# Casting the weight differences one block later, and forming the four sums of the second MLP's input in two steps

## The chip, the core and the metric

The program runs on one core of one Trainium2 chip. The metric is the device time of one execution in microseconds (us); lower is better. In the text PE is the matrix engine (TensorE), DVE is VectorE, ACT is ScalarE and POOL is GpSimd. Each engine works through its own queue in order; DVE, ACT and POOL hand results to each other and to PE through semaphores.

## What is computed

Rotary attention over 4 batches x 8 heads x 576 positions x 64, then two MLPs on its output, a matrix of 2304 x 512, all in float32:

```python
    gate = 1.0 / (1.0 + np.exp(-(x @ w_gate)))        # first MLP, d_ff 1536
    val = x @ w_val
    x = (gate * val @ w_out)
    h = x @ w_in                                      # second MLP, d_ff 2048
    g = h * (1.0 / (1.0 + np.exp(-1.702 * h)))
    return (g @ w_out).astype(np.float32)
```

The weights arrive as 64-bit numbers and are decoded to float32 on the chip.

## The kernel before

**Split products.** PE multiplies in the fp32r format, so each operand is held as a high part (a rounded copy) and a low part (the rest), and each product takes three matmuls: low x high, high x low, high x high (`split_mm`, L539; `product`, L614). The high part is made by a copy (ACT or DVE), the low part by a subtraction, mostly on POOL.

**Loops.** The hidden width is cut into chunks of 256 columns: six chunks (1, 0) to (1, 5) of the first MLP, eight chunks (2, 0) to (2, 7) of the second. The 2304 tokens are five blocks, 0 to 3 of 512 and 4 of 256. The order is written by hand: for a chunk, block after block, `hidden` (psum tiles `psh`, activation into `g`, L569 to L572) is issued, then the output product of an earlier block (`out1` or `out2`; psum tiles `pso`, added to `acc` by DVE, L693 or L710/L712), then the decoding of one piece of the next chunk's weights. There are four `psh` and four `pso` buffers: PE can run ahead of DVE by as much.

**A chunk of the second MLP** goes as follows. Blocks 0 and 1 are done together by `hidden_pair`: seven products of six matmuls, by a scheme that uses differences of the weight blocks (`Weights.differences`) and sums of the input blocks (`pair_sums`) in place of eight products. Then PE does, in this order, out2(4) of the chunk ahead, hidden(2), out2(0), hidden(3), out2(1), hidden(4), out2(2), out2(3), and the next chunk's pair. The numbers in brackets are blocks.

**Decoding.** `decode(i)` of a piece of 128x512: a copy on ACT into `wc` (L179), five DVE operations (L186 to L192; the last makes the high part of the weight), and POOL's subtraction for the low part (L210). Pieces 0 and 1 of a second-MLP chunk are the input weights; they stay in two `wt` buffers. With piece 1 (issued after out2(0) in a second-MLP chunk, after out1(0) in chunk (1, 5)) comes `differences`: four POOL subtractions on the two `wt` buffers (L202), then for each buffer a cast on ACT (L206) and a low part on POOL (L207). `wt` has two buffers in all, so piece 2 writes into the one that the first cast and its low part have read.

**The sums.** In chunk (1, 5) `out1` finishes the first MLP's output in `acc`. Behind out1(1) `pair_sums` forms four sums of 128x1024 on DVE (L601), casts each on ACT (L602) and makes each low part on POOL (L603). `hidden_pair` of chunk (2, 0) reads them.

Of the kernel before, what the change touches and what calls it, by code (L numbers as in the profile page):

```python
# [9 lines left out]
F32R = mybir.dt.float32r  # L10
U32 = mybir.dt.uint32
AF = mybir.ActivationFunctionType
ALU = mybir.AluOpType
# [13 lines left out]
def f(ap):  # L27
    return ap.bitcast(F32)
# [3 lines left out]
def attention_then_mlps(  # L32
# [86 lines left out]
            return a.rearrange("p (f w) -> p f w", w=2) if tag == "raw" else a  # L119

    stage = [Spare()]
    wpools = [big, None]
    wts = {}

    class Weights:
# [70 lines left out]
        def differences(self):  # L196
            t = [f(self.t.pop(i)) for i in range(2)]
            (b11, b12), (b21, b22) = [
                [a.rearrange("p (k f) -> p k f", k=2)[:, :, m * P : (m + 1) * P] for m in range(MT)] for a in t
            ]  # L200
            for dst, x, y in ((b11, b12, b11), (b12, b22, b12), (b22, b22, b11), (b21, b21, b22)):
                nc.gpsimd.tensor_tensor(dst, x, y, ALU.subtract)  # L202
            self.w[1] = self.half(wpools[0], 1)
            for i in range(2):
                w = self.w[1][:, :, i * PIECE : (1 + i) * PIECE]
                nc.scalar.activation(w[:, 0, :], t[i], AF.Copy)  # L206
                nc.gpsimd.tensor_tensor(w[:, 1, :], t[i], f(w[:, 0, :]), ALU.subtract)  # L207

        def lo(self, w, t):
            nc.gpsimd.tensor_tensor(w[:, 1, :], f(t), f(w[:, 0, :]), ALU.subtract)  # L210
# [377 lines left out]

    sums = []

    def pair_sums():
        sums.append(mlp["s"].tile([P, 2, 6, BLK], F32R, tag="sums", name="sums", bufs=1))
        a, b = (acc[n].rearrange("p (h c) -> p h c", h=2) for n in range(2))
        q = lambda t, e: t[:, :, e : e + 2, :].rearrange("p s e c -> p s (e c)")
        for out_, x, y, op, to in (
            (b[:, 1], b[:, 0], b[:, 1], ALU.add, q(xhl[1], 0)),
            (b[:, 0], a[:, 0], b[:, 0], ALU.subtract, q(sums[0], 2)),
            (a[:, 0], b[:, 1], a[:, 0], ALU.subtract, q(sums[0], 0)),
            (a[:, 1], a[:, 1], a[:, 0], ALU.subtract, q(sums[0], 4)),
        ):  # L600
            nc.vector.tensor_tensor(out_, x, y, op)  # L601
            nc.scalar.activation(to[:, 0], out_, AF.Copy)  # L602
            nc.gpsimd.tensor_tensor(to[:, 1], out_, f(to[:, 0]), ALU.subtract)  # L603

    def hidden_pair(W):
        g = [mlp["p"].tile([P, 2, MT, BLK], F32R, tag="g", name="g", bufs=3) for _ in range(2)]
# [73 lines left out]
    def out1(c, nchunk, W, n, g):  # L680
        if c == 0:
            acc[n] = new_f32(n, "acc")
        wd = width[n]
        if c == nchunk - 1:
            new_xhl(n)
        for e in range(KT):
            ps = mlp["ps_o"].tile([P, 512], F32, tag="pso", name="pso")
            split_mm(ps[:, :wd], lambda s, m: W.w_out(s, m, e * P, P), lambda s, m: g[:, s, m, :], MT)
            a = acc[n].rearrange("p (e w) -> p e w", w=wd)[:, e, :]
            if c == 0:  # L690
                nc.vector.tensor_copy(a, ps[:, :wd])
            else:
                nc.vector.tensor_tensor(a, ps[:, :wd], a, ALU.add)  # L693
            if c == nchunk - 1 and (n != 1 or e >= KT // 2):
                split_x(n, e, acc[n], nc.gpsimd)
        if c == nchunk - 1 and n == 1:
            pair_sums()

    def out2(c, nchunk, W, n, g):
        if c == 0:  # L700
# [128 lines left out]
    with tc.manual_schedule():  # L829
        load_first()  # L830
        for x in vtail:
            nc.gpsimd.memset(x, 0.0)
        nc.gpsimd.memset(least, -LARGEST)
        zeros = ps_t.tile([P, 512], F32, tag="pv", name="ps_w", bufs=1)

        def fill(n):
            for _ in range(n):
                nc.tensor.matmul(zeros[:, :P], vtail[1], vtail[1], start=True, stop=True)

        fill(20)  # L840
        wts[1, 0] = Weights(1, 0)
        ops = {
            "wm": lambda n, _: fill(n),
            "rm": lambda i, n, dve: rope_mul(i, n, nc.vector if dve else nc.gpsimd),
            "ra": rope_add,
            "t0": transpose_first,
            "hi": first_hi,
            "lo": first_lo,
            "st": first_stack,
            "rt": split_qk,  # L850
            "sh": second_hi,
            "sl": second_lo,
            "sd": second_stack,
            "sp": lambda *key: later.pop(("sp", *key))(),
            "xs": lambda *key: later.pop(("xs", *key))(),
            "sc": scores,
            "ex": exps,
            "no": inverse,
            "rs": spread,
            "pt": transpose_p,  # L860
            "pv": lambda i, n: pv(i, *PV_STEPS[n]),
            "ld": load,
            "lv": load_v,
            "lt": load_vtail,
        }
        for op, *args in FIRST:
            ops[op](*args)
        for G in range(FILL, NU * npairs + 20):
            slot(G)
            for n, (at_load, at) in enumerate(DEC):  # L870
                if G == at:
                    dec += wts[1, 0].decode(n, True)
                if G == at_load:
                    wts[1, 0].load(n)
            for (n, e), at in SPLIT.items():
                if G == at:
                    split_e(n, e)
            while early_steps and G == EARLY[early_steps[0]]:
                early_step(wts[1, 0], early_steps.pop(0))
            if G == NU * npairs - 1:  # L880
                rot.close()
                stage[0] = ctx.enter_context(
                    tc.tile_pool(name="stage_m", bufs=2, side="right", reuse_waits="tile")
                )
                mlp["x", 1] = ctx.enter_context(tc.tile_pool(name="xhl_a", bufs=1, side="right", reuse_waits="tile"))
                mlp["ps_h"] = ctx.enter_context(tc.tile_pool(name="ps_h", bufs=4, space=PSUM, side="right", reuse_waits="tile"))
        while dec:
            dec.pop(0)()
        soft.close()

        mlp["x", 2] = ctx.enter_context(tc.tile_pool(name="xhl_b", bufs=1, side="right", reuse_waits="tile"))
        mlp["p"] = ctx.enter_context(tc.tile_pool(name="mlp", bufs=1, reuse_waits="tile"))
        wpools[1] = mlp["p"]
        mlp["s"] = ctx.enter_context(tc.tile_pool(name="sums", bufs=1, reuse_waits="tile"))
        mlp["ps_o"] = ctx.enter_context(tc.tile_pool(name="ps_o", bufs=4, space=PSUM, reuse_waits="tile"))
        pend = []
        for at, (kind, c) in enumerate(chunks):
            nxt = chunks[at + 1] if at + 1 < len(chunks) else None
            share = [0] * NBLK
            if nxt:  # L900
                wts[nxt] = Weights(*nxt)
                if at:
                    wts[nxt].load(0)
                steps = [n for n in range(NBLK) if kind == 1 or n != 1]
                for i in range(wts[nxt].n):
                    share[steps[i % len(steps)]] += 1
            done = 0
            for n in range(NBLK):
                W = wts[kind, c]
                if at == 0 and n + 1 < NBLK:  # L910
                    split_block(n + 1)
                if at == n == 0:
                    for i in range(W.done, W.n):
                        if i not in W.raw:
                            W.load(i)
                        for op in W.decode(i):
                            op()
                    wts[nxt].load(0)
                if kind == 2 and n < 2:
                    gs = [] if n else hidden_pair(W)  # L920
                else:
                    gs = [hidden_rest(W) if at == n == 0 else hidden(kind, W, n)]
                for _ in range(len(pend) if kind == 1 or n == 0 else n > 1):
                    fn, *args = pend.pop(0)
                    fn(*args)
                for m, g in enumerate(gs):
                    pend.append((out1, c, FF1 // FFC, W, n + m, g) if kind == 1 else (out2, c, FF2 // FFC, W, n + m, g))
                for i in range(done, done + share[n]):
                    for op in wts[nxt].decode(i):
                        op()  # L930
                    if i + 1 < wts[nxt].n:
                        wts[nxt].load(i + 1)
                done += share[n]
                if kind == 2 and n == NBLK - 1:
                    fn, *args = pend.pop(0)
                    fn(*args)
        for fn, *args in pend:
            fn(*args)
# [108 lines left out]
```

## Time and profile before

| what | value |
|---|---|
| time, median of 3 runs | 1159.49 us (1159.13 to 1160.25) |
| profiled execution, its own time | 1159.3 us |
| its span, first to last instruction | 1157.5 us |
| PE busy | 1116.9 us, 96% of the span |
| DVE busy | 777.3 us, 67% |
| ACT busy | 439.5 us, 38% |
| POOL busy | 299.6 us, 26% |
| mean granted clock of PE | 0.992 of full speed |
| first MLP's last chunk and the pair after it | from about 655 to 746 us |
| second MLP's chunks with a chunk after them | from about 746 to 1112 us |

The profiled execution's time is 1.8 us above its span and 0.2 us below the median of the runs. Attention fills the first quarter of the span; the change touches nothing there. Busy shares are means over stages with different limits; what the change touches lies between 685 and 1112 us.

### The profile page before, as it was taken

The numbers are of one execution on the slowest core, as the hardware profiler recorded it, in microseconds if no ns is written. First come the engines' busy times: TensorE is split into PE (matmuls) and PEld (weight loads), VectorE is DVE, ScalarE is ACT, GpSimd is POOL, SyncE is SP. The second block draws the span as 40 slices with busy tenths as digits, with TensorE's granted clock in tenths as the row PEclk, the third lists the DMA queues.
The fourth block names the chain that finished last, engine by engine and source line by source line (L and its number), as shares of the span: only waits on it lengthen the run. The fifth ranks groups of instructions, "written<-read, shape, count | busy, mean of one in ns | idle before, by whom it ended". The sixth has DMA issues, their size and how long they took to land.

```text
span 1157.5 us, 15798 instructions
## 1 busy us (share of the span) xinstructions
PE 1116.9 (96%) x6048; PEld 930.1 (80%) x6048; DVE 777.3 (67%) x1356; ACT 439.5 (38%) x895; POOL 299.6 (26%) x277
## 2 busy tenths in 40 slices
PE   8999999999899999999999998989898989899898
PEld 8778888887788888888888887877787878787787
DVE  6887888776675555455555546767676766767664
ACT  6777777775331212122121123423232323223221
POOL 5445555422220101001010036431203122021200
PEclk9999999999999999999999999999999999999999
DMA  6676666621211111111111110011111111111114
GB/s 212 178 215 171 192 182 170 168 69 56 73 37 37 55 37 55 37 37 56 37 55 37 37 37 14 24 37 50 41 37 55 37 37 37 37 37 47 45 37 127
DMA packets 35803, 85.05 MB, mean 73 GB/s; under 512 B 6288, under 2 KB 11024, under 8 KB 33936
## 3 DMA queue, kind: packets, MB, share of 16 engines
q1 hardware_dynamic: 34912, 83.33, 24.8%
q8 instruction: 47, 0.77, 0.3%
q10 hardware_dynamic: 816, 0.72, 0.2%
q14 instruction: 28, 0.23, 0.1%
HBM read 60.44 MB, written 4.72 MB: 56 GB/s over the span
## 4 chain that ended last, share of the span: by engine, by line
PE 66%; DVE 22%; ACT 5%; POOL 3%; issue 3%; DMA 1%; SPq 0%; DVEq 0%; POOLq 0%; ACTq 0%
PE psh L539 23%; PE pso L539 17%; PE ps_x L508 5%; PE psh L614 5%; PE ps_p L477 5%; PE pss L405 4%; DVE acc L712 3%; PE pss L406 3%; DVE g L572 3%; ACT g L571 2%; DVE gf L570 2%; POOL wt L202 2%; DVE wt L188 2%; DVE g L649 2%; DVE wt L189 2%
## 5 line engine op out<-in xcount | busy, mean ns | idle before, releaser
L539 PE MATMUL psh<-xhl,w_in 128*128 128x512 f32 (+1 forms) x1968 | 406.0, 364 | 6.8 <-DVE gf L570 3.6
L539 PEld LDWEIGHTS psh<-xhl,w_in 128*128 128x128 f32 x1968 | 339.7, 190 | 66.8 <-DVE gf L570 3.8
L539 PE MATMUL pso<-w_out,g 128*128 128x512 f32 (+1 forms) x870 | 208.8, 396 | 23.4 <-DVE acc L712 19.0
L539 PEld LDWEIGHTS pso<-w_out,g 128*128 128x128 f32 x870 | 164.8, 192 | 61.9 <-DVE acc L712 22.7
L570 DVE TENSOR_TENSOR gf<-psh,gf 128x512 f32<-128x512 f32 (+1 forms) x108 | 66.6, 617 | 132.9 <-PE psh L539 81.5
L539 PE MATMUL pso<-g,w_out 128*128 128x512 f32 (+1 forms) x720 | 152.8, 368 | 0.0
L571 ACT ACTIVATE g<-gf 128x512 fp32r<-128x512 f32 (+1 forms) x108 | 62.3, 576 | 238.1 <-DVE gf L570 236.4
L210 POOL TENSOR_TENSOR w_in<-wt,w_in 128x512 fp32r<-128x512 f32 x38 | 49.8, 1311 | 384.1 <-DVE w_in L192 374.8
L539 PEld LDWEIGHTS pso<-g,w_out 128*128 128x128 f32 x720 | 125.8, 189 | 22.6
L408 DVE TENSOR_REDUCE nm<-pss 128x1 f32<-128x576 f32 x144 | 108.3, 753 | 32.0 <-PE pss L406 31.3
L572 DVE TENSOR_TENSOR g<-gf,g 128x512 fp32r<-128x512 f32 (+1 forms) x108 | 75.4, 698 | 69.4 <-ACT g L571 69.4
L569 ACT ACTIVATE gf<-psh 128x512 f32<-128x512 f32 (+1 forms) x108 | 57.7, 535 | 152.4 <-PE psh L539 151.7
L423 ACT ACTIVATE P<-pss,nm 128x576 f32<-128x576 f32 x128 | 94.9, 742 | 47.8 <-DVE nm L408 33.7
L210 POOL TENSOR_TENSOR w_out<-wt,w_out 128x512 fp32r<-128x512 f32 x28 | 36.2, 1293 | 237.9 <-DVE w_out L192 237.9
L712 DVE TENSOR_TENSOR acc<-pso,acc 128x512 f32<-128x512 f32 (+1 forms) x127 | 79.9, 679 | 8.7 <-PE pso L539 8.3
L295 POOL TENSOR_TENSOR x<-x,rope_sb 128x576 f32<-128x576 f32 x56 | 78.4, 1422 | 3.7 <-DMA x<-in_qk_dram 3.7
L477 PE MATMUL ps_p<-ident,P 128*128 128x128 f32 x576 | 78.4, 275 | 0.0
L693 DVE TENSOR_TENSOR acc<-pso,acc 128x512 f32<-128x512 f32 (+1 forms) x100 | 60.7, 633 | 23.0 <-PE pso L539 22.8
L477 PEld LDWEIGHTS ps_p<-ident,P 128*128 128x128 f32 x576 | 65.6, 140 | 8.0 <-issue 6.3
L508 PE MATMUL ps_x<-PT,v 128*64 128x320 f32 (+1 forms) x512 | 69.4, 412 | 0.0
L463 ACT ACTIVATE PT<-ps_p 128x512 f32<-128x512 f32 (+2 forms) x126 | 64.3, 535 | 4.4 <-PE ps_p L477 4.3
L179 ACT ACTIVATE wc<-raw 128x512 f32<-128x512 f32 x66 | 43.4, 657 | 40.4 <-DMA raw<-in_moe_w_gate_dram 33.6
(114 smaller groups left out, 1362.1 us busy)
## 6 DMA issues: line engine op xcount, KB each, us to landing
x<-in_qk_dram SPq DMA_DIRECT2D x14, 1152.0 KB, 6.0
raw<-in_moe_w_out_dram SPq DMA_DIRECT2D x28, 512.0 KB, 3.5
raw<-in_moe_w_in_dram SPq DMA_DIRECT2D x16, 512.0 KB, 3.6
raw<-in_moe_w_val_dram SPq DMA_DIRECT2D x12, 512.0 KB, 3.8
raw<-in_moe_w_gate_dram SPq DMA_DIRECT2D x10, 512.0 KB, 3.8
v<-in_v_dram SPq DMA_DIRECT2D x16, 256.0 KB, 3.4
Z<-X SPq DMA_DIRECT2D x14, 288.0 KB, 3.0
Z<-Y SPq DMA_DIRECT2D x14, 288.0 KB, 3.7
```

The source lines that it names most:

```text
L210: nc.gpsimd.tensor_tensor(w[:, 1, :], f(t), f(w[:, 0, :]), ALU.subtract)
L295: eng.tensor_tensor(x, x, rope_sb[:, t, c * S : (c + 1) * S], ALU.mult)
L408: nc.vector.tensor_reduce(nm, ps[:, :, :HALF], axis=AX.XY, op=ALU.max, negate=True)
L423: nc.scalar.activation(st[i]["P"][j][:, c : c + S].rearrange("p (n c) -> p n c", n=2), ps[:, :, :HALF], AF.Exp, bias=nm, accum_out=st[i][" ...
L463: nc.scalar.activation(dst, src, AF.Copy)
L477: nc.tensor.transpose(ps[:, (2 * x + y) * P : (2 * x + y + 1) * P], st[i]["P"][2 * a + y][:, c * P : (c + 1) * P], ident,)
L508: nc.tensor.matmul(ps[h * D : (h + 1) * D, :n], vt[:, h * MAINC + t, :], PT[:, h * (MAINC + 1) + t, :], start=False, stop=(t == MAINC - 1),)
L539: nc.tensor.matmul(ps, l(sl, a), r(sr, a), start=(sl == 1 and a == 0), stop=(sl + sr == 0 and a == n - 1))
L570: nc.vector.tensor_tensor(gf, pss[-1][:, :wd], gf, ALU.mult)
L571: nc.scalar.activation(g[:, 0, m, :], gf, AF.Copy)
L572: nc.vector.tensor_tensor(g[:, 1, m, :], gf, f(g[:, 0, m, :]), ALU.subtract)
L712: nc.vector.tensor_tensor(a, ps, a, ALU.add)
```

## The change

The two casts and the two low parts of `differences` become a function that is kept in a list and issued later: behind the next `hidden` that is issued, ahead of the output product of that block. The four subtractions on POOL stay where they were. `pair_sums` is called twice, behind out1(1) for the first two sums and behind out1(2) for the other two, and the low parts are made on DVE, each pair of them behind its two sums, in place of POOL.

```diff
     stage = [Spare()]
+    ready = []
...
             self.w[1] = self.half(wpools[0], 1)
-            for i in range(2):
-                w = self.w[1][:, :, i * PIECE : (1 + i) * PIECE]
-                nc.scalar.activation(w[:, 0, :], t[i], AF.Copy)
-                nc.gpsimd.tensor_tensor(w[:, 1, :], t[i], f(w[:, 0, :]), ALU.subtract)
+
+            def casts():
+                for i in range(2):
+                    w = self.w[1][:, :, i * PIECE : (1 + i) * PIECE]
+                    nc.scalar.activation(w[:, 0, :], t[i], AF.Copy)
+                    nc.gpsimd.tensor_tensor(w[:, 1, :], t[i], f(w[:, 0, :]), ALU.subtract)
+
+            ready.append(casts)
...
-    def pair_sums():
-        sums.append(mlp["s"].tile([P, 2, 6, BLK], F32R, tag="sums", name="sums", bufs=1))
+    def pair_sums(part):
+        if part == 0:
+            sums.append(mlp["s"].tile([P, 2, 6, BLK], F32R, tag="sums", name="sums", bufs=1))
...
-        for out_, x, y, op, to in (
+        todo = (
             (b[:, 1], b[:, 0], b[:, 1], ALU.add, q(xhl[1], 0)),
             (b[:, 0], a[:, 0], b[:, 0], ALU.subtract, q(sums[0], 2)),
             (a[:, 0], b[:, 1], a[:, 0], ALU.subtract, q(sums[0], 0)),
             (a[:, 1], a[:, 1], a[:, 0], ALU.subtract, q(sums[0], 4)),
-        ):
+        )[2 * part : 2 * part + 2]
+        for out_, x, y, op, to in todo:
             nc.vector.tensor_tensor(out_, x, y, op)
             nc.scalar.activation(to[:, 0], out_, AF.Copy)
-            nc.gpsimd.tensor_tensor(to[:, 1], out_, f(to[:, 0]), ALU.subtract)
+        for out_, x, y, op, to in todo:
+            nc.vector.tensor_tensor(to[:, 1], out_, f(to[:, 0]), ALU.subtract)
...
-        if c == nchunk - 1 and n == 1:
-            pair_sums()
+        if c == nchunk - 1 and n in (1, 2):
+            pair_sums(n - 1)
...
                     gs = [hidden_rest(W) if at == n == 0 else hidden(kind, W, n)]
+                if gs and ready:
+                    ready.pop()()
```

The first place is ACT's queue in a chunk of the second MLP, from the copy of piece 1 (`wc`) to the copy of piece 2. Before, the two casts (`w_in`) stand ahead of the activations of hidden(3) (`gf` and `g`):

```order
L179 ACTIVATE wc<-raw 128x512
L206 ACTIVATE w_in_7643<-wt 128x512 x2
L569 ACTIVATE gf<-psh 128x512
L571 ACTIVATE g<-gf 128x512
L569 ACTIVATE gf<-psh 128x512
L571 ACTIVATE g<-gf 128x512
L179 ACTIVATE wc<-raw 128x512
```

And in the changed kernel, in the same stretch:

```order
L180 ACTIVATE wc<-raw 128x512
L574 ACTIVATE gf<-psh 128x512
L576 ACTIVATE g<-gf 128x512
L574 ACTIVATE gf<-psh 128x512
L576 ACTIVATE g<-gf 128x512
L209 ACTIVATE w_in_7643<-wt 128x512 x2
L180 ACTIVATE wc<-raw 128x512
```

The casts have moved behind four activations and nothing else has changed its place; the same is so in all eight places of the program. POOL's queue keeps its order there, and DVE's too.

The second place is DVE's queue in chunk (1, 5), from the additions of out1(1) (`acc_4027` is block 1's, `acc_3910` block 0's, `acc_4143` block 2's) to the decoding of piece 3. Before, the four sums stand together:

```order
L693 TENSOR_TENSOR acc_4027<-pso,acc_4027 128x512 x4
L601 TENSOR_TENSOR acc_4027<-acc_4027 128x1024
L601 TENSOR_TENSOR acc_4027<-acc_3910,acc_4027 128x1024
L601 TENSOR_TENSOR acc_3910<-acc_4027,acc_3910 128x1024
L601 TENSOR_TENSOR acc_3910<-acc_3910 128x1024
L186 TENSOR_SCALAR wc<-wc 128x512
```

Now two sums and their two low parts stand there:

```order
L701 TENSOR_TENSOR acc_4027<-pso,acc_4027 128x512 x4
L608 TENSOR_TENSOR acc_4027<-acc_4027 128x1024
L608 TENSOR_TENSOR acc_4027<-acc_3910,acc_4027 128x1024
L611 TENSOR_TENSOR xhl_6766<-acc_4027,xhl_6766 128x1024
L611 TENSOR_TENSOR sums<-acc_4027,sums 128x1024
L187 TENSOR_SCALAR wc<-wc 128x512
```

The other two sums, with their low parts, have moved one block on, behind the additions of out1(2) and ahead of the decoding of piece 3:

```order
L701 TENSOR_TENSOR acc_4143<-pso,acc_4143 128x512 x4
L608 TENSOR_TENSOR acc_3910<-acc_4027,acc_3910 128x1024
L608 TENSOR_TENSOR acc_3910<-acc_3910 128x1024
L611 TENSOR_TENSOR sums<-acc_3910,sums 128x1024 x2
L187 TENSOR_SCALAR wc<-wc 128x512
```

DVE has four instructions more in all, POOL four fewer, and PE, the loads and the stores are the same.

## Rows read from the trace of the kernel before

**Rows 1.** PE's waits over the whole span: waited for, us in total, times, longest.

```profile
PE pso L539 <- DVE acc L712: 19.0, 12, 2.4
PE pso L539 <- DVE acc L710: 4.4, 2, 3.6
PE psh L539 <- DVE gf L570: 3.6, 1, 3.6
PE psh L614 <- ACT u L622: 1.3, 1, 1.3
```

**Rows 2.** Timeline of PE: start us, us, what, idle before; a middle chunk, the last chunk.

```profile
925.23 5.60 PE L539 MATMUL pso<-w_out,g 128*128 128x512 f32 x24
930.67 3.03 PE L539 MATMUL psh<-xhl,w_in 128*128 128x256 f32 x24
934.48 5.74 PE L539 MATMUL pso<-w_out,g 128*128 128x512 f32 x24 [0.78 <-DVE acc L712]
942.62 5.74 PE L539 MATMUL pso<-w_out,g 128*128 128x512 f32 x24 [2.39 <-DVE acc L712]
948.20 1.52 PE L614 MATMUL psh<-xhl,w_in 128*128 128x512 f32 x6
...
1112.30 2.88 PE L539 MATMUL pso<-w_out,g 128*128 128x512 f32 x12
...
1139.65 13.86 PE L539 MATMUL pso<-w_out,g 128*128 128x512 f32 x66
```

**Rows 3.** Stretches: length, busy time of each engine, PE's granted clock, DMA.

```profile
643.72:649.47 5.75, 5.75 (x50) 5.75 (x48) 4.52 (x8) 1.19 (x3) 1.29 (x1) 1.00 0.34 91
717.68:728.81 11.13, 7.50 (x50) 7.30 (x48) 9.40 (x13) 3.70 (x7) 4.89 (x3) 0.85 0.12 47
734.28:745.58 11.30, 9.97 (x43) 7.73 (x42) 8.23 (x15) 5.83 (x12) 6.32 (x5) 1.00 0.16 49
770.24:790.61 20.37, 15.98 (x73) 13.03 (x72) 15.67 (x28) 5.42 (x11) 5.52 (x5) 0.92 0.12 38
800.13:853.06 52.93, 49.75 (x224) 41.08 (x222) 36.96 (x64) 15.00 (x28) 10.62 (x10) 0.97 0.12 40
906.19:957.72 51.53, 48.35 (x224) 40.02 (x222) 36.77 (x64) 14.98 (x28) 10.61 (x10) 1.00 0.13 42
```

**Rows 4.** Timelines of POOL and of ACT around one chunk's casts.

```profile
924.12 1.29 POOL L210 TENSOR_TENSOR w_in<-wt,w_in 128x512 fp32r<-128x512 f32 x1 [7.79 <-DVE w_in L192]
925.37 3.20 POOL L202 TENSOR_TENSOR wt<-wt 128x256 f32<-128x256 f32 x4
928.53 2.56 POOL L207 TENSOR_TENSOR w_in<-wt,w_in 128x512 fp32r<-128x512 f32 x2
...
926.96 0.63 ACT L206 ACTIVATE w_in<-wt 128x512 fp32r<-128x512 f32 x1 [8.26 <-POOL wt L202]
```

**Rows 5.** Timeline of DVE in the same chunk.

```profile
923.62 0.43 DVE L192 CAST w_in<-wt 128x512 fp32r<-128x512 f32 x1
929.76 0.69 DVE L570 TENSOR_TENSOR gf<-psh,gf 128x512 f32<-128x512 f32 x1 [5.72 <-ACT gf L569]
...
933.75 2.48 DVE L712 TENSOR_TENSOR acc<-pso,acc 128x512 f32<-128x512 f32 x4
936.14 0.42 DVE L186 TENSOR_SCALAR wc<-wc 128x512 f32<-128x512 f32 x1
...
938.92 0.42 DVE L570 TENSOR_TENSOR gf<-psh,gf 128x256 f32<-128x256 f32 x1
939.82 0.90 DVE L572 TENSOR_TENSOR g<-gf,g 128x256 fp32r<-128x256 f32 x1 [0.48 <-ACT g L571]
...
941.88 2.48 DVE L712 TENSOR_TENSOR acc<-pso,acc 128x512 f32<-128x512 f32 x4
```

**Rows 6.** The sums' lines: ns min/median/max, first and last start.

```profile
L601 DVE TENSOR_TENSOR acc<-acc,acc x2: 1225/2290/3356, 707.3 to 708.6; 128x1024 f32<-128x1024 f32 x2
L603 POOL TENSOR_TENSOR sums<-acc,sums x3: 2577/3378/3390, 710.8 to 717.5; 128x1024 fp32r<-128x1024 f32 x3
```

## The prediction

> **What bounds the kernel now.** I first read what PE waits for. In the second MLP it is DVE's additions from `pso`: 19.0 us in 12 waits plus 4.4 us in 2, the fourteen being two in each of seven chunks; in the passage between the MLPs there are 3.6 us for `gf` and 1.3 us for ACT's `u` [rows 1]. So the bound is PE wherever it does not wait, and what the change can give back is the waits and what follows from them.
>
> What a chunk would take without waits comes from PE's timeline [rows 2]. The last chunk has no differences: from out2(4) to out2(2) it takes 1139.65 - 1112.30 = 27.35 us. Two more output products at 5.44 (930.67 - 925.23) and the pair at 9.52 (948.20, to 957.72 where the next chunk's stretch begins [rows 3]) make 47.75. The chunks take 52.93 (two of the six, to within 0.2) and 51.53 (the other four) [rows 3], so 5.18 and 3.78 are lost. That is more than the 0.78 + 2.39 of waits in a chunk [rows 2]: PE restarts more slowly behind a wait, and in the longer chunks its granted clock was 0.97, not 1.00. The sum is 2 x 5.18 + 4 x 3.78 = 25.5 us.
>
> The cause of the wait is read backwards in one chunk. PE begins out2(3) at 942.62, when DVE's first addition of out2(2), begun at 941.88, has emptied a buffer [rows 2, 5]. DVE runs without a gap from 929.76 to there, and ahead of 929.76 it sat idle for 5.72 us, for ACT's activation of hidden(3) [rows 5]. ACT was standing at the first cast, which waited 8.26 us for POOL's subtractions [rows 4]: these begin at 925.37, since piece 1 left DVE at 924.05 [rows 5] and POOL still had its low part to make. The activation's own input had been ready since before 925.23, when PE went on to out2(1) [rows 2]. So a queue order on ACT costs DVE 5.72 us, of which 3.78 reach PE.
>
> **The casts, in a steady chunk.** With the four activations ahead of the casts, DVE goes from 924.05 straight to hidden(3). Its four steps take 933.75 - 929.76 = 3.99 us [rows 5], to 928.0. They now lie beside POOL's subtractions, which they didn't before. The two low parts of `g` read two SBUF operands, and such an operation loses time beside POOL: one at 939.82 took 0.90, where the operation ahead of it, of the same size but with an operand in PSUM, took 0.42; and a sum of 128x1024 took 3.36 instead of 1.23, POOL's own subtraction 3.39 instead of 2.58 [rows 5, 6]. They take turns by whole instructions. One subtraction is 3.20 / 4 = 0.80 [rows 4], so each `g` waits up to that; from where the ends fall I take 0.3 for both together: 928.3. The first addition of out2(1) follows at once, the last must wait for PE, which ends out2(1) at 930.67 [rows 2]: DVE is free at 931.4. POOL, which gives two turns of 0.7, ends its subtractions at 925.37 + 3.20 + 1.4 = 930.0 or just before; the second cast ends at 930.6 and the two low parts of 2.56 [rows 4] at 932.5. DVE's decoding of piece 2 meets the last of them and starts about 1.0 late, at 932.4; it takes 938.92 - 936.14 = 2.78, hidden(4) takes 941.88 - 938.92 = 2.96 [rows 5], and the first addition of out2(2) ends 0.65 later, at 938.8. Without waits PE does hidden(4) and out2(2) from 930.67 to 930.67 + 2.87 + 5.44 = 938.98 and needs the buffer then. So no wait is left, with 0.1 us to spare, and all 25.5 us come back.
>
> The casts themselves cost nothing: ACT is busy 14.98 of 51.53 us [rows 3], and the weights, complete at 932.5 instead of 931.1, are read by PE with the pair, at 938.98 + 5.44 = 944.4. What is queued behind them on ACT is the copy of piece 2, which DVE takes up at 932.4; here lies the little cover there is.
>
> The other bound: POOL keeps the port through its whole run, and DVE's first `g` waits to 928.6, where the subtractions end (the casts are then behind that `g` on ACT, so POOL is idle). The remaining three steps end at 931.3, the additions at 933.7, decoding at 936.5, hidden(4) at 939.5, the first addition at 940.1: PE waits 1.1 us per chunk, 6.6 in six.
>
> **The first chunk, (2, 0).** From hidden(4) to the pair it takes 20.37 [rows 3] where 2.87 + 2 x 5.44 = 13.75 would do: 6.6 lost. Its first wait is 3.6 [rows 1] where the steady chunk has 0.78, so DVE is 2.8 later against PE there. With the 0.1 to spare 2.7 of waiting stays, and 3.9 come back. The granted clock was 0.92 in that stretch, which is 1.6 us of it; waits of 2.39 were followed by a lower clock in two chunks of six, so I count half of that as staying: 3.1.
>
> **The passage between the MLPs.** PE took 11.13 us for a stretch that, as chunk (1, 4)'s shows, takes 5.75 without a wait, and 11.30 for a pair of 9.52 [rows 3]: 5.4 + 1.8 = 7.2 lost. The 3.6 of waiting are for hidden(3)'s `gf` on DVE [rows 1]. DVE reaches it earlier by two sums that have moved on, up to 3.36 each there [rows 6], less two low parts of 1.23, which POOL now lets alone: some 4.2, and what hidden(2) gains from the later casts comes on top. So that wait goes. PE then starts the pair at 717.68 + 5.75 + 5.44 = 728.9 and, four products later, at 728.9 + 4 x 9.52 / 7 = 734.3, writes again into the buffer that ACT's `u` must have read. DVE's way there: PE ends out1(2) at 717.68, the last addition 0.8 later, at 718.5; two sums and two low parts at 1.23 are 4.9 alone, and 8.8 if three of them wait a turn of 1.29 for POOL's low parts of block 2 [rows 4, 6]; decoding 2.78; hidden(4) 2.96; four additions 2.4 [rows 5]; ACT's last cast and `u`, like the cast of 0.63 [rows 4], 1.3. That is 732.8 or 736.7, but the additions can't end before PE's out1(3), at 728.9, which they don't: a wait of nothing or of 2.4. The sum of 3.36 us was made under the same conditions, so I take 2.4, and 4.8 come back. The low parts moved to DVE (4 x 1.23) end by 727.3, the sums are first read at 730.3: hidden by hidden(4) and out1(3); without that cover they would cost their 4.9.
>
> The Trainium skill warns against just this move: its page Perfetto Trace Analysis, Optimizing Scalar/DVE Operations, says that VectorE and GpSimd share a port to SBUF and that moving work between the two may therefore not help. By that rule the 4.8 would be missing and the sum 28.6. The rows above bear out the turns, but also that DVE needs 1.23 where POOL needs 2.58 or more, so the work shrinks as it moves.
>
> **Sum.** 25.5 + 3.1 + 4.8 = 33.4 off the profiled execution's 1159.3: 1125.9. That execution lies 0.2 below the median of the runs, so I say 1126.
>
> **The rivals.**
> 1. POOL keeps the port through its run. For it: DVE loses up to 2.1 us on one instruction [rows 6]. Against: in the same rows POOL's instructions stretch too, so turns are taken. By the bound above: 25.5 - 6.6 = 18.9; in (2, 0) the wait grows to 3.8 and the clock's 1.6 stay, so 1.2; in the passage DVE is late in the same way, and 2 at most remain: 22 in all, 1137.
> 2. The sums' move gives nothing: 28.6, so 1131. What would carry it is that DVE's low parts run one after the other ahead of the decoding of piece 3, and the later half of the passage is DVE's alone: its 8.8 us there, made slower by one turn more for each of the two low parts and for the decoding, would end the additions 4 us later and use up the gain. It is what the page's rule would do, too.
> 3. The gain moves into DVE: it is the chain that set PE's pace, and what it no longer waits for at `gf` it waits for elsewhere, so that the chunk stays at 51.5. Against: DVE is busy 36.77 of 51.53 us [rows 3] and has 11 left under 47.75. About 1155 to 1160: no change.
> 4. Slower than before: the later casts hold the `wt` buffers. DVE's second operation of piece 2 writes into the buffer that the first low part reads; it stands ahead of hidden(4) and of PE's next buffer. That low part ends at about 931, and before, DVE came to it at 936.6. Only if it ended later than that, over 5 us beyond what I worked out, would the chunk be longer than before, and each further us costs 7 in seven chunks; 2 us more would be 1159 + 14 - 5 = 1168. POOL has nothing else in its queue, which speaks against it.
>
> **How the numbers follow.** Forecast 0.62; rival 1 0.18; rival 2 0.10; rival 3 0.03; rival 4 0.03; all waits gone (25.5 + 6.6 + 7.2 = 39.3 off, 1120) 0.04. The forecast, rival 1, rival 2 and the last hold over 9 in 10 between 1120 and 1138; I take these, since the turn-taking at the port, counted in tenths, decides whether a chunk waits at all. A measurement of this kernel tells 0.2%, 2.3 us, from no change. Faster by more has 0.94, within it 0.03, slower 0.03.
>
> **What the profile after should show.** Right: chunks from out2(4) to out2(4) of 47.7 to 48.1 us at a granted clock of 1.00; PE's waits for the additions down from 23.4 to under 5, with the largest left in (2, 0); DVE no longer idle for ACT's activation of hidden(3); the cast waiting for POOL by 2 us or less; `g` of hidden(3) at 0.7 to 1.5 us; the pair of (2, 0) still waiting some 2 us for `u`. A steady wait of about 1 at out2(3) would speak for rival 1; a passage as long as before for rival 2; a DVE idle at piece 2's second operation, for POOL, for rival 4. I am wrong if another wait stands ahead of out2(3) that the 5.72 covered, most likely piece 2's copy on ACT being late behind the casts.

## The result and the profile after

The changed kernel takes 1124.37 us (median of 4 runs, 1123.88 to 1125.18) beside 1159.36 for the kernel before in the same session. The ratio is 0.9697, 95% interval 0.9681 to 0.9714: faster by 3.0%. The forecast was 1126, range 1120 to 1138.

The page of the changed kernel: its span, and the chain that ended last by engine, in which DVE stood at 22% and PE at 66% before.

```profile
span 1123.4 us, 15790 instructions
...
PE 89%; DVE 6%; ACT 2%; issue 1%; POOL 1%; DMA 1%; DVEq 0%; POOLq 0%; ACTq 0%; SPq 0%
```

PE's waits for DVE and ACT from the last chunk of the first MLP on, columns as in [rows 1]. The fourteen waits for additions have become one; that for `gf` is gone, that for `u` has stayed.

```profile
PE pso L544 <- DVE acc L718: 2.0, 1, 2.0
...
PE psh L622 <- ACT u L630: 1.2, 1, 1.2
```

PE's timeline in a middle chunk, beside [rows 2]. hidden(4), out2(2) and out2(3) follow each other without a gap, the two output products now merged into one row of 48 matmuls:

```profile
906.03 5.60 PE L544 MATMUL pso<-w_out,g 128*128 128x512 f32 x24
911.48 3.04 PE L544 MATMUL psh<-xhl,w_in 128*128 128x256 f32 x24
914.35 11.07 PE L544 MATMUL pso<-w_out,g 128*128 128x512 f32 x48
925.25 1.52 PE L622 MATMUL psh<-xhl,w_in 128*128 128x512 f32 x6
```

The stretches that answer to [rows 3]: hidden(4) and out1(3) of chunk (1, 5); the pair; (2, 0) from hidden(4) to the next pair; two whole chunks.

```profile
718.82:730.04 11.22, 11.22 (x74) 10.26 (x73) 10.85 (x10) 4.23 (x7) 6.56 (x4) 1.00 0.00 0
730.04:741.21 11.17, 9.99 (x44) 7.73 (x42) 8.11 (x15) 5.84 (x12) 6.32 (x5) 1.00 0.15 49
765.87:781.92 16.05, 14.08 (x74) 11.81 (x73) 14.38 (x25) 3.54 (x8) 6.32 (x6) 1.00 0.16 47
791.44:839.22 47.78, 47.78 (x224) 40.04 (x223) 37.49 (x64) 15.43 (x28) 11.66 (x10) 1.00 0.15 44
887.00:934.77 47.77, 47.77 (x223) 40.05 (x222) 37.47 (x64) 15.30 (x28) 11.65 (x10) 1.00 0.15 45
```

The chunks take 47.78 us where 47.75 was worked out as the length without waits, at full clock; all six lie between 47.77 and 47.79. From these rows the time that came back is: in six chunks 312.17 - 286.68 = 25.5 us; in (2, 0) 20.37 - 16.05 = 4.3; in the passage, from hidden(4) of (1, 5) to the end of the pair, 27.90 - 22.39 = 5.5. These are 35.3. The span is 34.1 shorter: hidden(4) of (1, 5) begins at 718.82 instead of 717.68, because the stages ahead of it, attention above all, took 1.1 longer in this execution.

POOL, ACT and DVE in the same chunk, beside [rows 4, 5]:

```profile
904.93 1.29 POOL L215 TENSOR_TENSOR w_in<-wt,w_in 128x512 fp32r<-128x512 f32 x1 [7.80 <-DVE w_in L193]
906.18 4.25 POOL L203 TENSOR_TENSOR wt<-wt 128x256 f32<-128x256 f32 x4
910.39 2.56 POOL L210 TENSOR_TENSOR w_in<-wt,w_in 128x512 fp32r<-128x512 f32 x2
...
907.65 0.63 ACT L576 ACTIVATE g<-gf 128x512 fp32r<-128x512 f32 x1 [0.76 <-DVE gf L575]
908.29 0.63 ACT L209 ACTIVATE w_in<-wt 128x512 fp32r<-128x512 f32 x1
910.46 0.63 ACT L209 ACTIVATE w_in<-wt 128x512 fp32r<-128x512 f32 x1 [1.53 <-POOL wt L203]
...
904.77 0.68 DVE L575 TENSOR_TENSOR gf<-psh,gf 128x512 f32<-128x512 f32 x1
906.15 0.69 DVE L577 TENSOR_TENSOR g<-gf,g 128x512 fp32r<-128x512 f32 x1 [0.70 <-ACT g L576]
...
911.68 0.69 DVE L720 TENSOR_TENSOR acc<-pso,acc 128x512 f32<-128x512 f32 x1 [0.67 <-PE pso L544]
912.28 0.94 DVE L187 TENSOR_SCALAR wc<-wc 128x512 f32<-128x512 f32 x1
...
918.55 2.48 DVE L720 TENSOR_TENSOR acc<-pso,acc 128x512 f32<-128x512 f32 x4
```

DVE goes to hidden(3)'s `gf` at 904.77 without the 5.72 of idle time. The first cast waits for nothing, the second 1.53. POOL's four subtractions take 4.25 instead of 3.20, since they give turns to DVE; DVE's `g` loses nothing at 906.15, and the first operation of piece 2 takes 0.94 instead of 0.42. The first addition of out2(2) begins at 918.55 and takes some 0.65, to 919.2; PE needs its buffer at 914.35 + 5.44 = 919.79.

### The profile page after: what moved, and what is told of

Same layout as the page of the kernel before. It is cut to its first block, busy times and chain, and to the rows that moved or that the text cites. A ratio compares the mean times of both kernels' runs of the same rounds, so it can differ in the third digit from the quotient of the medians.

```text
span 1123.4 us, 15790 instructions
## 1 busy us (share of the span) xinstructions
PE 1106.0 (98%) x6048; PEld 924.3 (82%) x6048; DVE 783.6 (70%) x1360; ACT 441.6 (39%) x895; POOL 297.2 (26%) x273
## 4 chain that ended last, share of the span: by engine, by line
PE 89%; DVE 6%; ACT 2%; issue 1%; POOL 1%; DMA 1%; DVEq 0%; POOLq 0%; ACTq 0%; SPq 0%
PE psh L544 33%; PE pso L544 28%; PE psh L622 6%; PE ps_x L513 5%; PE ps_p L482 5%; PE pss L410 4%; PE pss L411 3%; PE ps_x L510 1%; DVE nm L413 1%; PE ps_r L453 1%; PE ps_p L497 1%; PE ps_w L846 0%; DVE wt L189 0%; ACT xhl L107 0%; ACT g L576 0%
## 5 line engine op out<-in xcount | busy, mean ns | idle before, releaser
L544 PE MATMUL pso<-w_out,g 128*128 128x512 f32 (+1 forms) x870 | 201.5, 388 | 2.0 <-DVE acc L718 2.0
L544 PEld LDWEIGHTS pso<-w_out,g 128*128 128x128 f32 x870 | 162.0, 188 | 35.4 <-DVE acc L718 2.4
L413 DVE TENSOR_REDUCE nm<-pss 128x1 f32<-128x576 f32 x144 | 108.3, 754 | 31.8 <-PE pss L411 31.1
```

Source lines behind the costliest of these rows:

```text
L413: nc.vector.tensor_reduce(nm, ps[:, :, :HALF], axis=AX.XY, op=ALU.max, negate=True)
L544: nc.tensor.matmul(ps, l(sl, a), r(sr, a), start=(sl == 1 and a == 0), stop=(sl + sr == 0 and a == n - 1))
```

## The experiments

The theory and the rivals are those of the prediction. Each kernel was timed in five rounds beside the kernel before, which had a median of 1159.57, 1159.78 and 1160.53 in the three sessions. Executions of one kernel differ by 1 to 7 us, and hidden(4) of (1, 5) begins between 717.4 and 719.9 us into the profiled ones, so small differences are read from the stretches behind that point, not from the times.

**The casts alone.** The changed kernel with `pair_sums` as before:

```diff
-        if c == nchunk - 1 and n in (1, 2):
-            pair_sums(n - 1)
+        if c == nchunk - 1 and n == 1:
+            pair_sums()
```

> The casts are issued one block later, the four sums stay as before (one step behind out1(1), low parts on POOL). My theory: the seven chunks of the second MLP gain in full, so their length is 47.8 us and the stretch of (2, 0) from hidden(4) to the pair stays near 16 us: some 29.8 of the 35 us. In the passage DVE begins the sums only about 1.7 us earlier against PE than before, so the wait of 3.6 for hidden(3)'s gf shrinks to about 1.9 and stays: 1127 to 1128 us. Rival (the sums' move gives nothing): no psh wait is left and the time is that of the whole change, 1124.4.

It took 1128.48 us, ratio 0.9737 (0.9720 to 0.9754). Chunks are 47.78, (2, 0) 16.05 as in the whole change. PE's waits:

```profile
PE pso L544 <- DVE acc L715: 2.0, 1, 2.0
PE psh L544 <- DVE gf L575: 1.9, 1, 1.9
PE psh L619 <- ACT u L627: 1.6, 1, 1.6
PE psh L619 <- DVE gf L575: 0.9, 1, 0.9
```

The `gf` wait is 1.9, as worked out, and a second wait in the pair is 0.9. The passage takes 26.19 us, 3.8 more than with the sums moved. So the casts bring 31, of which 1.7 lie in the passage (26.19 where it took 27.90 before), and the sums' move is worth about 4. That speaks against rival 2, by which it gives nothing.

**The sums alone.** The kernel before with the changed `pair_sums` and its two calls:

```diff
-        if c == nchunk - 1 and n == 1:
-            pair_sums()
+        if c == nchunk - 1 and n in (1, 2):
+            pair_sums(n - 1)
```

> The sums in two steps with low parts on DVE, the casts as before. My theory: chunks of 51.5 to 53 us and DVE idle 5.7 us for hidden(3) in each, as before; in the passage the psh wait of 3.6 goes, the pair's wait for u stays: about 5 us off, 1154. Rival (the sums' move gives nothing, or only together with the casts): 1159.

It took 1155.41 us, ratio 0.9962 (0.9950 to 0.9974): 4.2 off. PE's waits for the additions are those of before [rows 1]:

```profile
PE pso L539 <- DVE acc L715: 18.9, 12, 2.4
PE pso L539 <- DVE acc L713: 4.4, 2, 3.6
PE psh L617 <- ACT u L625: 1.7, 1, 1.7
PE psh L617 <- DVE gf L570: 0.8, 1, 0.8
```

The six chunks take 312.15 us in all and (2, 0) 20.38, as before. The wait for `gf` in front of hidden(4) is gone without the casts' help, and the passage takes 23.87 instead of 27.90. 31.1 and 4.2 make 35.3, the whole change is 35.0: the two parts add up.

**The low parts on POOL, in two steps.** One line of the changed kernel:

```diff
-            nc.vector.tensor_tensor(to[:, 1], out_, f(to[:, 0]), ALU.subtract)
+            nc.gpsimd.tensor_tensor(to[:, 1], out_, f(to[:, 0]), ALU.subtract)
```

> The whole change, but the low parts of the sums stay on POOL, in two steps. My theory: DVE has 4.9 us less to do, but the decoding of pieces 2 and 3 meets POOL's low parts of 2.4 each and loses 1 to 2 us on each, and POOL's last low parts end near where the pair begins; a wait of up to 1 us for the sums can come in. 1124 to 1127. Rival (moving work between the two engines cannot help, since they share a port): no difference from the whole change, 1124.4.

It took 1129.23 us, ratio 0.9740 (0.9723 to 0.9757), more than either expectation. PE waits 3.1 in the pair for `gf` of hidden(4), and the passage is 26.19 again. DVE and POOL at the decoding of piece 3:

```profile
726.17 5.11 POOL L611 TENSOR_TENSOR sums<-acc,sums 128x1024 fp32r<-128x1024 f32 x2
...
725.49 1.02 DVE L187 TENSOR_SCALAR wc<-wc 128x512 f32<-128x512 f32 x1 [1.68 <-ACT wc L180]
726.54 2.50 DVE L188 TENSOR_SCALAR wt<-wc 128x512 uint32<-128x512 uint32 x1
729.08 2.75 DVE L189 SCALAR_TENSOR_TENSOR wt<-raw,wt 128x512 uint32<-128x512 uint32 x1
731.86 0.69 DVE L190 SCALAR_TENSOR_TENSOR wt<-wc,wt 128x512 uint32<-128x512 uint32 x1
```

Operations of 0.43 and 0.69 become 2.50 and 2.75: each waits for most of a POOL instruction of some 2.5 and then runs. DVE, spared 2.46 of its own low parts there, loses 4.7 on three operations. So moving the low parts to DVE pays because a long POOL instruction can cost DVE nearly its own length at the port. The Trainium skill (SBUF — State Buffer, Who interferes with whom) says that a VectorE operation with two SBUF inputs contends with a GpSimd operation that reads SBUF, that one in a mode that uses both of VectorE's ports contends too, and that whichever issues first holds the shared ports for its whole instruction. These rows agree. The Trainium skill's advice that moving work between the two may not help (Perfetto Trace Analysis, Optimizing Scalar/DVE Operations) is not borne out here: the move is worth 3.8 us in the passage.

The times differ by more, 4.9 us. In the profiled execution (2, 0) took 17.69 instead of 16.05: out2(3) there ran at a granted clock of 0.76, behind a wait of 2.0 that in the changed kernel was followed by 5.74 us at 1.00.

```profile
779.04 7.34 PE L544 MATMUL pso<-w_out,g 128*128 128x512 f32 x24 [2.02 <-DVE acc L718]
```

**Both steps behind out1(1), low parts on DVE.**

```diff
-        if c == nchunk - 1 and n in (1, 2):
-            pair_sums(n - 1)
+        if c == nchunk - 1 and n == 1:
+            pair_sums(0)
+            pair_sums(1)
```

> The whole change, but both steps of the sums stand behind out1(1), low parts on DVE. By the durations in the trace after, eight operations of 1.23 from 705.5 end at 715.3 with POOL idle, hidden(3) reaches its first buffer at 718.8, before PE needs it at 720.2, and the additions of out1(3) and u are some 2 us earlier than with two steps: the psh wait is gone and the wait for u too. 1122.5 to 1124.4. Rival (making the sums in two steps is what removes the psh wait): a wait of 1 to 3 us for gf comes back, 1126 to 1128.

It took 1124.93 us, ratio 0.9702 (0.9686 to 0.9718), the same as the change within the measurement. There is no `psh` wait, and the passage takes 22.30 instead of 22.39. So the two steps are not what helps; the engine of the low parts is. The four kernels with the later casts form a square, here by the length of the passage: low parts on POOL in one step and in two, then on DVE in one step and in two.

```profile
718.03:744.22 26.19, 21.71 (x116) 17.96 (x114) 20.25 (x31) 10.82 (x21) 13.65 (x11) 1.00 0.14 41
717.68:743.87 26.19, 21.49 (x116) 17.91 (x114) 21.28 (x26) 11.19 (x20) 18.39 (x11) 1.00 0.07 21
719.58:741.88 22.30, 21.20 (x116) 17.99 (x115) 16.91 (x26) 10.42 (x21) 12.06 (x10) 1.00 0.11 37
718.82:741.21 22.39, 21.21 (x116) 17.99 (x114) 18.97 (x24) 10.07 (x19) 12.88 (x9) 1.00 0.07 25
```

The wait for `u` was 1.1, against my expectation: DVE waited 1.26 for piece 3's copy on ACT, which stood behind the casts of block 2, and its decoding then met POOL's low parts of block 2 (1.40 and 1.67 for operations of 0.43 and 0.69).

**More DVE work in piece 2.** The clamp of piece 2 is repeated once, or four times, and changes nothing in the result:

```diff
+            return ops[:2] + ([ops[1]] * 1 if self.kind == 2 and i == 2 else []) + ops[2:]
```

> The whole change, with the clamping operation of piece 2 done once more on DVE in each second-MLP chunk (0.42 us and the gap to the next, some 0.47; the result is unchanged by it). It measures the cover ahead of out2(3). In the trace after, the first addition of out2(2) ends near 919.2 and PE would need it at 919.8, so about 0.6 is spare: chunks stay at 47.8, only (2, 0), which waits already, grows by 0.5: 1124.9. If only the 0.1 is spare that the prediction worked out, each of six chunks loses about 0.4: 48.1 to 48.2 and 1127.

> As with one clamping operation more, but four more: some 1.9 us. With 0.6 spare each chunk should wait about 1.3 at out2(3): chunks of 49.1, in six 7.8, with (2, 0)'s 1.9 a time of 1134, and more where the granted clock falls behind the wait. Rival (DVE's chain sets the pace of the chunk, so that nothing is spare): 1.9 in each, 49.7 and 1137.5.

With one, 1126.09 us (0.9710, 0.9696 to 0.9724); chunks of 47.84 to 47.86 without a wait in the list. The time lies between the two that were expected, 1124.9 and 1127; the chunks are those of the first, and the passage and (2, 0) are longer by 0.3 and 0.5. With four, 1139.07 (0.9825, 0.9811 to 0.9840); chunks of 49.21 to 49.28 and in each a wait of 1.15:

```profile
PE pso L545 <- DVE acc L721: 6.9, 6, 1.2
PE pso L545 <- DVE acc L719: 3.7, 1, 3.7
```

0.47 costs a chunk 0.07, 1.9 costs it 1.45: by the chunk's length 0.4 to 0.5 is spare ahead of out2(3), and beyond that the chunk is DVE's. By the wait it is some 0.7 (1.9 less 1.15); the other 0.3 is PE's slower restart behind a wait, as in the chunks before, where at full clock two waits of 3.17 together cost 3.78. The 1134 expected for four was too low, because six chunks lost 8.8 instead of 7.8, because piece 2 of (2, 0)'s own weights is decoded in the passage and got the clamps too (24.07 for 22.39), and because in (2, 0) the wait of 3.7 and what follows it cost 4.5 instead of 1.9 (20.56 for 16.05).

**POOL later with the first cast's low part.** It is done five times, with the same result:

```diff
-                    nc.gpsimd.tensor_tensor(w[:, 1, :], t[i], f(w[:, 0, :]), ALU.subtract)
+                    for _ in range(1 if i else 5):
+                        nc.gpsimd.tensor_tensor(w[:, 1, :], t[i], f(w[:, 0, :]), ALU.subtract)
```

> The whole change, with POOL's low part behind the first cast done five times (5.2 us more of POOL on the first of the two wt buffers; the result is unchanged by it). This is the rival that ends slower: the casts hold wt. The first low part now ends near 911.7 in the chunk where DVE's second operation of piece 2 begins at 913.3, so 1.6 are spare; with 5.2 more DVE must wait 3.6, and up to 1.3 more for the port, and PE, behind the 0.6 that is spare there, 3 to 4.3 per chunk: 18 to 26 in six and 4 to 5 in (2, 0), 1146 to 1155. If the buffers do not hold DVE, no change: 1124 to 1126.

It took 1176.79 us, ratio 1.0147 (1.0128 to 1.0166): slower than before. DVE in one chunk, PE's waits, and a whole chunk:

```profile
943.06 1.50 DVE L188 TENSOR_SCALAR wt<-wc 128x512 uint32<-128x512 uint32 x1 [3.92 <-POOL w_in L211]
```

```profile
PE pso L545 <- DVE acc L721: 25.7, 6, 4.3
PE pso L545 <- DVE acc L719: 7.1, 1, 7.1
```

```profile
1076.72:1131.32 54.60, 50.32 (x223) 41.59 (x222) 38.90 (x64) 15.41 (x28) 16.84 (x14) 0.94 0.10 30
```

DVE waits for the buffer as rival 4 says, 3.92 and about 1.1 at the port, and PE waits 4.28. The chunk grows by 6.8 and not by 4.3: the granted clock falls to 0.94, and PE is busy 2.5 us longer (50.32 instead of 47.78). The expected 1146 to 1155 was therefore far too low: the six chunks lost 41.2 us where 18 to 26 were expected, (2, 0) 7.6 where it was 4 to 5, and the passage, for which nothing was expected, 4.2. The mechanism is real; in the changed kernel DVE's wait lies about 1.6 us of POOL time away (the first low part ends near 911.7, DVE comes at 913.33), PE's some 0.6 more.

**u first.** The casts of block 3 go behind `u` on ACT:

```diff
+            if c == nchunk - 1 and n == 3:
+                ready.append(lambda e=e: split_x(3, e, acc[3], nc.gpsimd))
...
         nc.scalar.activation(u, X, AF.Copy)
+        while ready:
+            ready.pop(0)()
```

> The whole change, and the cast of block 3 of the first MLP's output moved behind u on ACT (in the pair of (2, 0)). My theory: the wait for u (1.2, and 1.65 of the pair's length with its restart) goes, since X is ready about 4 us before u now starts: the pair takes 9.5 to 9.8 and the time is 1122.7 to 1123.3. Rival: the wait moves to the additions on DVE that stand ahead of V5 and Z, and the pair keeps its length: 1124.4.

It took 1125.22 us, ratio 0.9704 (0.9688 to 0.9720): no gain. The passage is 21.07, 1.3 less, with no wait for `u`. But DVE comes to the buffer of out2(3) only some 0.3 us earlier, so in (2, 0) PE waits longer, and behind the wait it runs more slowly (granted clock 0.76):

```profile
777.05 7.38 PE L544 MATMUL pso<-w_out,g 128*128 128x512 f32 x24 [2.94 <-DVE acc L722]
```

**u first, and two copies of out2(0) on ACT.**

```diff
+                if c == n == 0 and t > 1:
+                    nc.scalar.activation(a, ps, AF.Copy)
+                elif c == 0:
```

> The kernel with u first, and in chunk (2, 0) two of the four copies of out2(0) out of psum made on ACT instead of DVE. With u first the 1.3 us won in the pair came back as a longer wait at out2(3) of (2, 0) (2.94 for 1.97) and a lower granted clock behind it, since DVE is late there. Two copies are 1.2 us of DVE: if DVE's lateness is the cause, that wait is about 1.7, the clock stays full and the time is 1.3 to 1.6 us below that of the change, 1122.8 to 1123.1. Rival: the copies on ACT put off the activation of piece 1 and so DVE, and nothing is gained: 1124.4 to 1125.2.

> The changed kernel once more, on the same chip as the last one, to compare the two: 1124.4, with chunks of 47.8.

They took 1123.86 (0.9678, 0.9662 to 0.9693) and 1124.62 us (0.9687, 0.9670 to 0.9704), not to be told apart. The wait is 1.8, near the 1.7 expected, but the clock did not stay full. out2(3) of (2, 0) in the new kernel, and in the change run again, where a wait of 1.9 stood ahead of it:

```profile
774.31:781.53 7.22, 7.22 (x25) 5.76 (x25) 6.19 (x11) 0.00 (x0) 1.29 (x1) 0.76 0.24 73
```

```profile
775.29:780.87 5.58, 5.58 (x25) 4.61 (x25) 5.37 (x10) 0.00 (x0) 0.98 (x1) 1.00 0.17 40
```

In these two executions the 1.3 won in the pair goes into the 1.6 of lower clock. No version beat the change by more than the measurement tells.

## Why the prediction was right

The predicted 1126 was right, and so was its mechanism; the terms of the sum, one by one:

- **The steady chunks:** 25.5 predicted, 25.5 measured. The chain as read backwards (ACT's queue, then `gf`, then the additions, then `pso`) was the cause: the casts alone bring it, the sums alone nothing of it. Its details were off with no effect on the sum. POOL gave turns, 4.25 for its subtractions where 4.6 was worked out, but `g` lost nothing and piece 2 lost 0.5 instead of 1.0. So 0.4 to 0.7 is spare, by the trace and by the added clamps, where 0.1 was predicted.
- **(2, 0):** 3.1 predicted, 4.3 measured. The wait that stays is 2.0 instead of 2.7, and the granted clock stayed at 1.00; the half of 1.6 that I counted for it was not lost in this execution. That part is luck: behind a wait of the same 2.0 all of it was lost with the low parts on POOL, and behind waits of 1.8 and 2.9 in the last experiments, but not behind 2.0 with the casts alone or 1.9 in the change run again.
- **The passage:** 4.8 predicted, 5.5 measured. Three of DVE's four operations behind out1(2) waited a turn, as worked out, but of 1.0 to 1.1 instead of 1.29: two sums of 2.36 and 2.21 and two low parts of 3.46 together, where each takes 1.23 alone. They ended at 727.5, where 728.4 had been worked out (727.3, and 1.1 for the later start of this passage). The wait for `u` was 1.2 instead of 2.4. Not all of it is the sums' doing: 1.5 to 1.7 come from the casts (27.90 to 26.19, and 23.87 to 22.39), which the prediction let come on top without a size, and 3.8 to 4.0 from the sums.

```profile
719.62 2.36 DVE L608 TENSOR_TENSOR acc<-acc,acc 128x1024 f32<-128x1024 f32 x1
722.02 2.21 DVE L608 TENSOR_TENSOR acc<-acc 128x1024 f32<-128x1024 f32 x1
724.15 3.46 DVE L611 TENSOR_TENSOR sums<-acc,sums 128x1024 fp32r<-128x1024 f32 x2
```

- **Rival 1 (POOL keeps the port)** is refuted by the chunks' length and by the turns in the low-parts experiment. **Rival 2** (the sums' move gives nothing) is refuted by the casts alone (26.19 for 22.39) and by the sums alone (23.87 for 27.90). **Rival 3** (the chunk stays at DVE's pace) is refuted by chunks of 47.78. **Rival 4** (the casts hold the `wt` buffers) is a true mechanism, but POOL ends too early for it here. The prediction's price for it was too low. It let POOL end over 5 us later before a chunk is as long as before, and POOL's four extra operations of 1.3 made it 54.6 us for 51.5: DVE's turn at the port (1.1) and PE's lower clock (busy 50.32 for 48.35) were not counted.
- **The reason given for two steps was not needed.** I had the `gf` wait go because two sums move on a block. In one step with the low parts on DVE it goes as well: what made the sums slow before was POOL's low parts beside them, 3.36 instead of 1.23. In two steps with the low parts on POOL it goes too, but 3.1 of waiting come back in the pair.

The sum of the three terms was 33.4 and came to 35.3; the 1.1 ahead of the passage took part of the difference back in the profiled execution.

## What to carry to other kernels

Look for an in-order engine that stands at an instruction whose input comes from a slow engine, with work behind it that was ready long ago; moving that one instruction behind the ready work can free the engine after next. Before costing such a move, follow it to the buffer that PE waits for and compare two numbers, how much earlier the chain ends and how much earlier PE needs it, since only the smaller one comes back. And of VectorE and GpSimd, try the one that does an operation in shorter instructions (here 1.23 us against 2.4 to 2.6): an instruction of the other lost up to 2.1 us beside one of 2.6.

## What the runs showed of the hardware that was not expected

- Of two operations that meet at the port it is sometimes POOL that pays: in the steady chunk its four subtractions took 4.25 instead of 3.20 while DVE's `g` of 128x512 stayed at 0.69. With long POOL instructions DVE pays: 2.50 and 2.75 for operations of 0.43 and 0.69.
- A wait of PE of about 2 us is followed by a lower granted clock in some executions (0.76 over the 7.2 us behind waits of 1.8 and 2.0) and not in others (1.00 behind 1.9 and 2.0). In the kernel with the low parts on POOL the passage with its wait of 3.1 even stayed at 1.00, and the slower stretch came behind the wait of 2.0. What decides it stays open.
- Once nothing waits, six chunks of 47.78 us agree within 0.02 us; the 2.5 us by which the start of hidden(4) of (1, 5) differs between the profiled executions come from ahead of it, mostly from attention, whose code is the same in all of them.
